# Attention, channel mix and gated MLP on one core: a reordered opening, and query features spread by DMA

## The chip, the cores and the metric

The kernel runs on one core of a Trainium2 chip. The metric is device time in microseconds of one execution. TensorE multiplies matrices, VectorE (DVE), ScalarE (ACT) and GpSimd (POOL) work on elements, and SyncE (SP) issues the DMAs of the kernel before.

## The reference

Three layers follow each other, for 4 batches of 1088 positions, in float32:

```python
# 1. linear attention, 4 heads of 32, r = 8
phi(x)[s, 8*i + j] = (S1 @ x[s])[i] * (S2 @ x[s])[j]      # 64 features per head
q_p, k_p = phi(q), phi(k)
kv = sum_s k_p[s, f] * v[s, d];   z = sum_s k_p[s, f]
x  = (q_p @ kv) / (q_p @ z + 1e-6)                        # heads side by side: 128 channels
# 2. channel mix
xk = mu_k * x + (1 - mu_k) * x_prev;   xr = mu_r * x + (1 - mu_r) * x_prev
x  = sigmoid(xr @ w_r) * (relu(xk @ w_k) ** 2 @ w_v)      # 128 -> 1024 -> 128
# 3. gated MLP with a mix over positions
h = relu(x @ w_in);  u, v = halves of h;  v_n = layernorm(v)
out = (u * (w_spatial @ v_n + b_spatial)) @ w_out
```

## The kernel before, in words

**Number formats.** Most large products are three fp32r matmuls: both factors are split in a high and a low part, and `mm3` (L111) multiplies low by high, high by high and high by low. An fp32 matmul on unsplit operands is one instruction in the program and two records in the profile. The weights arrive as 64-bit numbers; `load64` issues the load (L147) and `conv64` converts one piece to high and low parts with some five VectorE instructions (L124 to L129), two or three of ScalarE and one of GpSimd (L132). Three raw buffers take turns, so the fourth load waits for the first conversion.

**Chunks.** The 1088 positions of a batch are three chunks of 384, 384 and 320; `i` = 0 to 11 counts the chunks of all batches. Attention and channel mix go chunk by chunk, and the last layer follows per batch.

**Attention of a chunk.** `k_feat` computes key features: three fp32 matmuls of 128 positions (L188) give the two projections, with positions on partitions, and an outer product on VectorE or GpSimd (L199) gives 256 features. `k_sum` adds features times values over the nine tiles of a batch (L219; the mask is L224). `q_feat` does the same as `k_feat` for queries. `q_turn` transposes the features by six TensorE transposes (L240) and two ScalarE copies, so that features lie on partitions. `q_num` multiplies them with the key sums (L257) and divides (L261 to L263). `q_out` transposes back (L275). `prep` mixes a chunk with its shifted copy and splits it (L296 to L300), `prep_r` does so for the gate.

**Channel mix.** One step `g` is one of eight 128-wide pieces of a chunk: `up(g)` is an `mm3` and a ReLU (L339), `sqsplit(g-1)` the square, `down(g-4)` the down-projection. A piece is of one of two kinds: "P" squares on GpSimd (L342), makes the high part on ScalarE (L371) and the low part on VectorE, and needs an `mm3` in `down`; "D" squares on ScalarE (L359) and needs one fp32 matmul with the total of the value weights `wvT` (L385). Kinds alternate, P for even pieces. At a chunk's last piece VectorE multiplies by the gate (L389). 96 steps make up the loop; `plan(g, fn, ...)` hangs other work on a step: the features, turn, numerators and way back of chunk j at steps `QS[j]` and after (a new chunk every seven steps), key features of the next batch, weight loads and conversions.

**Order.** The program is traced in this order, and a planner that simulates the engines then sets each engine's order; `behind(anchors, fn)` makes all instructions of `fn` come after the given ones on the same engine. DMAs are issued by SP in order.

**The opening.** The loads go out in this order: the projections, keys of batch 0 (L166), the first half of the up-weights (L147), the first query chunk (L173), values of batch 0 (L177), constants, the second half of the up-weights, keys of batch 1, and so on. Eleven matmuls on zeros (L556) come first on TensorE. Then: key features of batch 0, features of query chunk 0, key sums, turn, numerators, way back, `prep(0)`, key features of batch 1 on GpSimd, key sums of batch 1, and the loop.

Of the kernel before, what the change touches and what calls it, by code (L numbers as in the profile page):

```python
# [12 lines left out]
ALU = mybir.AluOpType  # L13
# [18 lines left out]
CONVP = (512,)  # L32
NWARM = 11
VP = 2 * (HD + 1)
G1 = 26
WS = 30
WR = 2.5
C0 = 17
CS = 6
EARLY = 4  # L40
KB1 = ("w4", "w5", "w6")
QP = (3, 4, 6, 9, 10)
KP = (6, 10)
QJ = (0, 0, 4, 1, 0, -4, -1, 0, 2, 2, 0, -8)
PG = 1
ES = 93
EP = 2
# [12 lines left out]
ORD0 = ((0, 0), (1, 0), (0, 1), (1, 1), (2, 0), (3, 0), (2, 1), (3, 1), (0, 2), (1, 2), (2, 2), (3, 2))  # L60
R0 = (1, 4, 5)
R1 = 5
VW = NH * (HD + 1)
# [3 lines left out]
def attn_moe_gmlp(ctx: ExitStack, tc: tile.TileContext, qT, kT, va, st, wk, wv, wr, win, wout,  # L67
# [4 lines left out]
    pool = ctx.enter_context(tc.tile_pool(name="sb", bufs=1))  # L72
    pp = ctx.enter_context(tc.tile_pool(name="ps", bufs=1, space=PSUM))

    uid = [0]
# [128 lines left out]
    def k_feat(b, c, pb=4, eng=None):  # L204
        kp = kps[b, c] = sb((KB1 if b == 1 else ("n0H", "n0L", "n1H"))[c], [128, 3, 256])
        features(k_s[b], c, kp, pb, GE if 3 * b + c in KP else eng, eng is not None)

    def k_sum(b, g, ts=range(NT)):
        if g == 0 and ts[0] == 0:
            kps[b] = bank(3 if b == 1 else 5)  # L210
        kv = kps[b]
        v8 = v_s[b][0].rearrange("p t h c -> p t (h c)")
        v9 = v_s[b][1].rearrange("p h c -> p (h c)")
        wide = b % 2 == 0
        w = VW if wide else VP
        for t in ts:
            kp = kps[b, t // 3][:, t % 3, 128 * g:128 * g + 128]
            vt = v8[:, t] if t < NK else v9
            TE.matmul(kv[:, w * g:w * g + w], lhsT=kp, rhs=vt if wide else vt[:, VP * g:VP * g + VP],  # L219
                      start=(t == 0), stop=(t == NT - 1))  # L220
        if g == 1:
            nh = w // (HD + 1)
# [4 lines left out]
            kbd[b] = kb.rearrange("p (g h) c -> p g (h c)", g=2)  # L227

    def q_feat(i):
        qp = qst[i] = sb("n1L", [128, 3, 256])  # L230
        features(q_s[i // 3], i % 3, qp, 4, GE if i in QP else None)

    def q_turn(i):
        c = i % 3
        n = CH[c][1]
# [95 lines left out]
    def up(g):  # L331
# [6 lines left out]
        r = sb(rot(*R), [128, n])  # L338
        SE.activation(out=r, in_=hk, func=AF.Relu)  # L339
        if kind(g) == "P":  # L340
            sq = sb(rot(*R), [128, n])
# [7 lines left out]

    def kind(g):  # L350
        p = PAT[(g >= G1) + (g >= G2)]
        return p[g % len(p)]

    def sqsplit(g):
        i, f = divmod(g, NF)
        n = CH[i % 3][1]
        if kind(g) == "D":
# [19 lines left out]
    def down(g):  # L377
# [5 lines left out]
        w = slice(128 * f, 128 * f + 128)  # L383
        if kind(g) == "D":
            TE.matmul(vvs[i], lhsT=wvT[:, f // 2], rhs=hls.pop(g), start=f == 0, stop=f == NF - 1)  # L385
        else:
# [96 lines left out]
    def spatial(b, d, c, fill, early=False):  # L483
# [34 lines left out]
        def tail():  # L518
            mm3(po[c], woH[:, ds], woL[:, ds], gH, gL, rank == 1, rank == ND)
            if rank == ND:  # L520
# [28 lines left out]
    winH, winL = sb("winH", [128, DFF], F32R), sb("winL", [128, DFF], F32R)  # L549
    woH, woL = sb("woH", [128, DG], F32R), sb("woL", [128, DG], F32R)  # L550
    T2s = [sb(f"T2{d}", [128, 128], F32R) for d in range(ND)]
    zero = sb("mx", [128, CMAX], F32R)
    VE.memset(zero.bitcast(F32), 0.0)
# [20 lines left out]
    wseq += [(win, winH, winL, o, CV) for o in range(0, DFF, CV)]  # L574
    wseq += [(wout, woH, woL, o, CV) for o in range(0, DG, CV)]
    wi = [0]
# [17 lines left out]

    load64(*wseq[0])
    load_q(0, (0,))
    load_v(0)
    nc.sync.dma_start(out=idn, in_=ident)
    nc.sync.dma_start(out=mus[:, 0:2], in_=mu)
    VE.tensor_scalar(out=mus[:, 2:3], in0=mus[:, 0:1], scalar1=-1.0, scalar2=1.0, op0=ALU.mult, op1=ALU.add)  # L600
    load64(*wseq[1])
    load_k(1)
    load64(*wseq[2])
    load_v(1)
    load_q(0, (1, 2))
    for c in range(NCH):
        k_feat(0, c, c)
    k_last = outer[0]

    def behind(anchors, fn, *a):  # L610
        with ExitStack() as es:
            for x in anchors:
                es.enter_context(tc.issue_after(x.ins))
            fn(*a)

    q_feat(0)
    k_sum(0, 0)
    k_sum(0, 1)
    k_mask0 = list(k_mask)
    q_turn(0)  # L620
# [8 lines left out]
    k1_last = outer[0]  # L629
    behind([k_last], conv64)  # L630
    load64(*wseq[3])
    behind(nd_pe0, k_sum, 1, 0, range(3))
    behind(x_turn0, k_sum, 1, 0, range(3, NT))
    k_sum(1, 1)
    behind(k_mask0 + [k1_last], conv64)
    load64(*wseq[4])
    load_q(1)
# [6 lines left out]
    def gated(fn):  # L644
        return wraps(fn)(lambda *a: behind(prep_0, fn, *a))

    NI = B * NCH
# [12 lines left out]
    for b in range(1, B):  # L660
        last = QS[3 * b]
        ks = (3, 6, 8) if b == 1 else (last - 19, last - 12, last - 5)
        for c in range(NCH if b > 1 else 0):
            plan(ks[c], k_feat, b, c)
        if b > 1:
            plan(last + 1, k_sum, b, 0)
            plan(last + 2, k_sum, b, 1)
        if b + 1 < B:
# [8 lines left out]

    def total_wv(h):
        H, L = [x.bitcast(F32).rearrange("p (f two d) -> p f two d", two=2, d=128)[:, 2 * h:2 * h + 2, 1] for x in (wvH, wvL)]
        GE.tensor_tensor(out=wvT[:, 2 * h:2 * h + 2], in0=H, in1=L, op=ALU.add)  # L680
# [9 lines left out]
    plan(R1 + 1, receive, 0)  # L690
    plan(R1 + 2, gate, 0)
    for n, x in enumerate(wseq[5:]):
        plan(C0 - 2 + CS * n, load64, *x)
        plan(C0 + CS * n, conv_late)
# [27 lines left out]
    ds = slice(DG - 128, DG)  # L722
    GE.tensor_tensor(out=wo_last, in0=woH[:, ds].bitcast(F32), in1=woL[:, ds].bitcast(F32), op=ALU.add)
    at[0] = NI * NF + 1
# [86 lines left out]
```

## Time and profile before

| | |
|---|---|
| three runs | 474.67 us median, 473.85 to 474.92 |
| profiled execution | 475.52 us, its span 473.7 us |
| TensorE busy | 456.4 us, 96% |
| VectorE, ScalarE busy | 235.6 us (50%), 236.3 us (50%) |
| GpSimd busy | 189.9 us (40%) |
| first up-projection | at 27.12 us |

The profile's span is the time between the first and the last instruction that it shows. Busy times are sums over instructions; a matmul's end is modelled, so overlapping matmuls can hide small gaps. A line such as L111 is that of a helper and stands for many places; the names of its operands tell them apart.

### The profile page before, as it was taken

To read this page: it belongs to the slowest core of one execution; us is meant where nothing else is said; L and a number is where in the kernel's file an instruction comes from. 1 tells how busy PE (TensorE), PEld (TensorE's weight loads), DVE (VectorE), ACT (ScalarE), POOL (GpSimd) and SP (SyncE) were. 2 spreads that over 40 slices of the span, in tenths; PEclk is the share of its full clock that TensorE was granted. 3 is DMA by queue.
4 is the path that set the end of the run, shared out by engine and by line. 5 is a ranking of instruction groups with operands and counts; after the bars stand their busy time and mean duration, and the time that the engine had idled before them with its cause. 6 is when DMAs were issued, how large, how long until landed. Compare 5 with 4: busy or idle time off the path is not lost.

```text
span 473.7 us, 7304 instructions
## 1 busy us (share of the span) xinstructions
PE 456.4 (96%) x2754; PEld 433.4 (91%) x2754; DVE 235.6 (50%) x433; ACT 236.3 (50%) x569; POOL 189.9 (40%) x247
## 2 busy tenths in 40 slices
PE   6987999989999999999999999999999999999997
PEld 5976899788998898899999999999999999999996
DVE  3778748788477774437552335621335521212121
ACT  2464687886786866876435423432523442311111
POOL 2447545576475785456325503341213440200000
PEclk9899999999999999999999999999999999999999
DMA  7952200112200000022000000000100000100001
GB/s 239 335 192 91 92 1 19 33 35 77 66 19 0 2 0 1 0 72 80 26 17 18 0 15 0 1 2 0 48 1 1 1 1 0 48 1 0 1 1 47
DMA packets 12228, 18.77 MB, mean 40 GB/s; under 512 B 1761, under 2 KB 10785, under 8 KB 12193
## 3 DMA queue, kind: packets, MB, share of 16 engines
q1 hardware_dynamic: 12192, 18.31, 12.3%
q8 instruction: 21, 0.34, 0.3%
q14 instruction: 15, 0.11, 0.1%
HBM read 16.08 MB, written 2.23 MB: 39 GB/s over the span
## 4 chain that ended last, share of the span: by engine, by line
PE 71%; DVE 9%; ACT 6%; DMA 5%; POOL 4%; issue 3%; SPq 1%; POOLq 0%; DVEq 0%; ACTq 0%
PE p L111 59%; DMA st<-in_wT_dram 3%; PE p L385 3%; DVE w L117 3%; PE p L219 2%; PE p L257 2%; PE p L507 2%; PE p L508 2%; ACT m L339 2%; DMA xs0H<-in_va_dram 2%; PE p L188 1%; DVE w L127 1%; ACT w L114 1%; DVE m L117 1%; ACT w L371 1%
## 5 line engine op out<-in xcount | busy, mean ns | idle before, releaser
L512 DVE TENSOR_TENSOR m<-p,m 128x384 f32<-128x384 f32 (+1 forms) x43 | 22.9, 532 | 96.9 <-PE p L508 92.7
L111 PE MATMUL p<-m,k 128*128 128x384 f32 (+1 forms) x288 | 65.4, 347 | 2.7 <-ACT m L339 2.7
L342 POOL TENSOR_TENSOR m<-m 128x384 f32<-128x384 f32 (+1 forms) x48 | 41.3, 863 | 46.9 <-ACT m L339 43.2
L499 ACT ACTIVATE m<-p 128x384 f32<-128x384 f32 (+1 forms) x44 | 20.6, 469 | 77.2 <-PE p L111 73.4
L111 PEld LDWEIGHTS p<-m,k 128*128 128x128 f32 x288 | 47.8, 189 | 6.9 <-ACT m L339 3.7
L111 PE MATMUL p<-w,m 128*128 128x384 f32 (+1 forms) x288 | 52.3, 327 | 0.0
L111 PE MATMUL p<-w,k 128*128 128x384 f32 (+1 forms) x288 | 51.6, 327 | 0.0
L111 PE MATMUL p<-w,n1H 128*128 128x384 f32 (+1 forms) x192 | 48.7, 330 | 1.0 <-DVE x L512 1.0
L111 PEld LDWEIGHTS p<-w,m 128*128 128x128 f32 x288 | 48.1, 188 | 0.5
L111 PE MATMUL p<-w,n0H 128*128 128x384 f32 (+1 forms) x192 | 48.2, 329 | 0.0
L111 PEld LDWEIGHTS p<-w,k 128*128 128x128 f32 x288 | 47.9, 188 | 0.3
L339 ACT ACTIVATE m<-p 128x384 f32<-128x384 f32 (+1 forms) x96 | 42.9, 473 | 9.5 <-PE p L111 8.9
L117 DVE TENSOR_TENSOR w<-m,w 128x384 fp32r<-128x384 f32 (+1 forms) x44 | 33.4, 771 | 26.5 <-ACT w L371 21.7
L117 DVE TENSOR_TENSOR m<-m,m 128x384 fp32r<-128x384 f32 (+1 forms) x47 | 27.2, 578 | 28.8 <-ACT m L114 27.6
L111 PEld LDWEIGHTS p<-w,n1H 128*128 128x128 f32 x192 | 34.2, 188 | 2.4 <-DVE x L512 1.3
L453 POOL TENSOR_SCALAR rs<-mv 128x1 f32<-128x1 f32 x34 | 8.4, 246 | 66.0 <-DVE mv L452 65.1
L111 PEld LDWEIGHTS p<-w,n0H 128*128 128x128 f32 x192 | 34.2, 188 | 0.5
L385 PE MATMUL p<-w,wvT 128*128 128x384 f32 (+1 forms) x88 | 34.5, 474 | 0.1
L447 ACT ACTIVATE VR<-p 128x512 f32<-128x512 f32 x34 | 20.2, 597 | 27.7 <-PE p L111 27.6
L111 PE MATMUL p<-w,n0L 128*128 128x384 f32 (+1 forms) x96 | 31.5, 328 | 0.0
L111 PE MATMUL p<-w,n1L 128*128 128x384 f32 (+1 forms) x96 | 31.5, 328 | 0.0
L455 DVE TENSOR_SCALAR VR<-VR,mv,rs 128x512 f32<-128x512 f32 x34 | 21.1, 621 | 20.4 <-POOL rs L454 20.4
(193 smaller groups left out, 1042.9 us busy)
## 6 DMA issues: line engine op xcount, KB each, us to landing
st<-in_wT_dram SPq DMA_DIRECT2D x16, 192.0 KB, 2.4
w<-in_kT_dram SPq DMA_DIRECT2D x8, 192.0 KB, 4.5
w<-in_qT_dram SPq DMA_DIRECT2D x8, 192.0 KB, 3.9
out_dram<-m SPq DMA_DIRECT2D x8, 192.0 KB, 1.9
st<-in_wT_dram SPq DMA_DIRECT2D x8, 160.0 KB, 2.3
xs0H<-in_va_dram SPq DMA_DIRECT2D x2, 528.0 KB, 7.0
xs0L<-in_va_dram SPq DMA_DIRECT2D x2, 528.0 KB, 4.4
w<-in_wk_dram SPq DMA_DIRECT2D x2, 512.0 KB, 6.2
```

Source lines behind the costliest of these rows:

```text
L111: TE.matmul(out_ap, lhsT=l, rhs=r, start=first and n == 0, stop=last and n == 2)
L117: return eng.tensor_tensor(out=L, in0=src, in1=H.bitcast(F32), op=ALU.subtract)
L219: TE.matmul(kv[:, w * g:w * g + w], lhsT=kp, rhs=vt if wide else vt[:, VP * g:VP * g + VP], start=(t == 0), stop=(t == NT - 1))
L257: nd_pe[0] = TE.matmul(o.rearrange("p h c -> p (h c)"), lhsT=qt[g][:, cut(c, t)], rhs=kb[:, g], start=not wide or g == 0, stop=not wide or ...
L339: SE.activation(out=r, in_=hk, func=AF.Relu)
L342: anchor[2] = GE.tensor_tensor(out=sq, in0=r, in1=r, op=ALU.mult)
L385: TE.matmul(vvs[i], lhsT=wvT[:, f // 2], rhs=hls.pop(g), start=f == 0, stop=f == NF - 1)
L447: SE.activation(out=v, in_=pv, func=AF.Relu)
L455: VE.tensor_scalar(out=v, in0=v, scalar1=mv[:, 0:1], scalar2=rs, op0=ALU.subtract, op1=ALU.mult)
L499: SE.activation(out=u, in_=pu, func=AF.Relu)
L507: TE.matmul(acc, lhsT=T2, rhs=wtile(NK, c)[1], start=False, stop=False)
L512: VE.tensor_tensor(out=u, in0=acc, in1=u, op=ALU.mult)
```

## The change

It has three parts.

- **Opening.** The first query chunk and the values of batch 0 are asked for before the up-weights; keys and values of batch 1 come after four of the weight loads. Eight filler matmuls on zeros stand between the query features of chunk 0 and the key sums, twelve more behind the first transpose of the way back. The conversions of both up-weight and both value-weight pieces are done before the loop, each behind a step of the chain. Key features and key sums of batch 1 move from the opening into the loop (steps 4, 6 and 8 for the features), with VectorE for the outer product. The gate of chunk 0 is prepared at step 1 where it was step 5.
- **Unsplit squares in chunk 0.** All eight pieces use one fp32 matmul: even ones are squared by GpSimd ("G"), odd ones by ScalarE ("D"). The totals of the even value-weight pieces go to `wvE`, in the place of the output weights' high part, which are loaded and converted later.
- **Query features of chunks 3 to 11.** One matmul with a reordered projection gives all 64 + 32 values (both factors of four heads) of a chunk with positions along the free dimension; ScalarE copies them to SBUF and issues a DMA to a buffer in DRAM; SP issues six DMAs that read them back, each row repeated over eight partitions, as the two factors of all 256 features with features on partitions; one product on VectorE or GpSimd makes the features in the place where the turned ones stood. The spread is issued three steps earlier than the features were (for chunks 3 to 9; at their old step for 10 and 11) and is pinned behind the last square, split and low part of the loop on their engines.

```diff
+NFILL = (8, 12)
+KS1 = (4, 6, 8)
+SPREAD = 3
+QE_ = 3
-R0 = (1, 4, 5)
-R1 = 5
+R0 = 2
+R1 = 1
 ...
     def k_feat(b, c, pb=4, eng=None):
-        kp = kps[b, c] = sb((KB1 if b == 1 else ("n0H", "n0L", "n1H"))[c], [128, 3, 256])
-        features(k_s[b], c, kp, pb, GE if 3 * b + c in KP else eng, eng is not None)
+        kp = kps[b, c] = sb(("n0H", "n0L", "n1H")[c], [128, 3, 256])
+        features(k_s[b], c, kp, pb, GE if 3 * b + c in KP else None)
 ...
+    def q_order():
+        t = sb("T12", [128, 2, 2 * NH, 8])
+        for x in range(2):
+            GE.tensor_copy(t[:, x], Sb[:, :, 8 * x:8 * x + 8])
+        Sq[0] = t.rearrange("p s h i -> p (s h i)")
+
+    def q_spread(i):
+        b, c = divmod(i, 3)
+        o, n = CH[c]
+        e = rot(1, 0)
+        pq = bank(6 + e)[:, :n]
+        TE.matmul(pq, lhsT=Sq[0], rhs=q_s[b][:, o:o + n], start=True, stop=True)
+        y = vr(8, n)[:96]
+        copy(y, pq[:96])
+        fa = VR[:, 2 * e:2 * e + 2, :n]
+        fb = VR[:, 6:8, :n] if e else sb("n1L", [128, 2, n])
+        far = dp.tile([96, n], F32, tag=f"far{e}", bufs=1, name=f"far_{i}")
+        nc.scalar.dma_start(out=far, in_=y)
+        for h in range(NH):
+            r, g = 8 * h, h // 2
+            if h % 2 == 0:
+                nc.sync.dma_start(out=fa[:, g], in_=far[r:r + 16].unsqueeze(1).to_broadcast([16, 8, n]))
+            nc.sync.dma_start(out=fb[64 * (h % 2):64 * (h % 2) + 64, g],
+                              in_=far[64 + r:72 + r].unsqueeze(0).to_broadcast([8, 8, n]))
+        qst[i] = (fa, fb)
+
+    def q_prod(i):
+        fa, fb = qst[i]
+        (GE if i in QP else VE).tensor_tensor(out=fa, in0=fa, in1=fb, op=ALU.mult)
+        qst[i] = [fa[:, 0], fa[:, 1]]
 ...
+        if kind(g) == "G":
+            sq = sb(rot("w4", "w5", "w6", "w7"), [128, n])
+            anchor[2] = GE.tensor_tensor(out=sq, in0=r, in1=r, op=ALU.mult)
+            hls[g] = sq
+            return
 ...
     def kind(g):
+        if g < NF:
+            return "GD"[g % 2]
 ...
-        if kind(g) == "D":
-            TE.matmul(vvs[i], lhsT=wvT[:, f // 2], rhs=hls.pop(g), start=f == 0, stop=f == NF - 1)
+        if kind(g) in "DG":
+            TE.matmul(vvs[i], lhsT=(wvT if f % 2 else wvE)[:, f // 2], rhs=hls.pop(g), start=f == 0, stop=f == NF - 1)
 ...
-    load64(*wseq[0])
     load_q(0, (0,))
     load_v(0)
     nc.sync.dma_start(out=idn, in_=ident)
+    load64(*wseq[0])
+    load64(*wseq[1])
     nc.sync.dma_start(out=mus[:, 0:2], in_=mu)
-    VE.tensor_scalar(out=mus[:, 2:3], in0=mus[:, 0:1], scalar1=-1.0, scalar2=1.0, op0=ALU.mult, op1=ALU.add)
-    load64(*wseq[1])
-    load_k(1)
+    GE.tensor_scalar(out=mus[:, 2:3], in0=mus[:, 0:1], scalar1=-1.0, scalar2=1.0, op0=ALU.mult, op1=ALU.add)
     load64(*wseq[2])
-    load_v(1)
     load_q(0, (1, 2))
 ...
+    def busy(i, n):
+        p = bank(i)[:, :CMAX]
+        for x in range(n):
+            TE.matmul(p, lhsT=zero[:, :128], rhs=zero, start=x == 0, stop=x == n - 1)
+
     q_feat(0)
+    q_last = outer[0]
+    busy(7, NFILL[0])
+    behind([q_last], conv64)
+    load64(*wseq[3])
+    load64(*wseq[4])
+    load_k(1)
+    load_v(1)
     k_sum(0, 0)
     k_sum(0, 1)
     k_mask0 = list(k_mask)
+    behind(k_mask0, conv64)
     q_turn(0)
     q_num(0)
     nd_last0 = list(nd_last)
     nd_pe0 = list(nd_pe)
+    behind(nd_last0, conv64)
     q_out(0)
-    x_turn0 = list(x_turn)
+    behind(x_turn[:1], busy, 3, NFILL[1])
     prep(0)
-    for c in range(NCH):
-        k_feat(1, c, c, GE)
-    ...
-    k_sum(1, 1)
-    ...
+    behind(prep_L[:1], conv64)
     load_q(1)
 ...
-            plan(QS[j] + sp * n, gated(fn) if j < 3 and n == 0 else fn, j)
+            early = QE_ if SPREAD <= j < 10 and n == 0 else 0
+            plan(QS[j] + sp * n - early, gated(fn) if j < 3 and n == 0 else pinned(fn) if j >= SPREAD and n == 0 else fn, j)
 ...
-    for n in range(3):
-        plan(R0[n], conv_first)
-        if n < 2:
-            plan(R0[n], total_wv, n)
+    for n in range(2):
+        for odd in range(2):
+            plan(3 * n, total_wv, n, odd)
+    plan(R0, conv_first)
+    plan(QS[SPREAD] - QE_ - 3, q_order)
     plan(R1, prep_r, 0)
```

## Rows read from the trace of the kernel before

**Rows 1.** The page: busy time, share and instructions of each engine.

```profile
PE 456.4 (96%) x2754; PEld 433.4 (91%) x2754; DVE 235.6 (50%) x433; ACT 236.3 (50%) x569; POOL 189.9 (40%) x247
```

**Rows 2.** By stretch: length, busy (count) of PE, PEld, DVE, ACT, POOL, clock, DMA, GB/s.

```profile
30.00:40.00 10.00, 6.87 (x52) 6.26 (x51) 9.23 (x16) 9.28 (x22) 4.62 (x6) 1.00 0.44 131
...
80.00:100.00 20.00, 17.94 (x116) 16.06 (x114) 14.81 (x24) 15.61 (x41) 12.21 (x12) 1.00 0.14 40
100.00:120.00 20.00, 19.05 (x116) 16.23 (x117) 16.66 (x25) 16.09 (x41) 13.04 (x12) 1.00 0.23 65
```

**Rows 3.** TensorE's waits by releaser: us in total, times, longest.

```profile
PE p L111 <- ACT m L339: 2.7, 4, 1.3
...
PE p L240 <- DVE n1L L199: 1.7, 1, 1.7
PE p L275 <- DVE VR L263: 1.6, 2, 1.4
...
PE p L188 <- ACT sab L114: 0.9, 1, 0.9
PE p L240 <- POOL n1L L199: 0.7, 1, 0.7
```

**Rows 4.** The chain of waits, in order of time: start, us, what.

```profile
11.30 5.97 PE p L219 x36
...
45.99 0.52 PE p L111 x3
...
101.20 0.65 PE p L240 x6
101.85 0.67 PE p L188 x6
102.70 0.65 PE p L385 x2
...
125.66 0.54 PE p L385 x2
```

**Rows 5.** Timeline of TensorE in the opening: start, us, operation.

```profile
15.74 0.84 PE L219 MATMUL p<-xs0H,n0L 128*128 128x132 f32 x6
16.41 0.61 PE L219 MATMUL p<-xs0H,n1H 128*128 128x132 f32 x4
...
19.75 1.52 PE L257 MATMUL p<-kb,VR 128*128 128x132 f32 x12
...
25.14 1.95 PE L219 MATMUL p<-xs0L,w 128*128 128x66 f32 x16
26.92 0.39 PE L219 MATMUL p<-va,w 128*128 128x66 f32 x2
27.12 1.83 PE L111 MATMUL p<-m,k 128*128 128x384 f32 x9
```

**Rows 6.** Table by stretch of one microsecond in the opening.

```profile
8.00:9.00 1.00, 0.00 (x0) 0.00 (x0) 0.00 (x0) 0.00 (x0) 0.00 (x0) 1.00 1.04 378
...
12.00:13.00 1.00, 1.00 (x6) 1.00 (x6) 1.00 (x2) 0.00 (x0) 0.00 (x0) 0.50 0.98 301
```

**Rows 7.** The page's costliest groups: busy, mean ns of one, idle before.

```profile
L339 ACT ACTIVATE m<-p 128x384 f32<-128x384 f32 (+1 forms) x96 | 42.9, 473 | 9.5 <-PE p L111 8.9
```

**Rows 8.** Timeline of SP: start, us, DMA issue.

```profile
3.99 0.43 SPq L177 DMA_DIRECT2D xs0H<-in_va_dram  x1
```

**Rows 9.** DMA issues by form: KB each, us from issue to landing.

```profile
st<-in_wT_dram SPq DMA_DIRECT2D x16, 192.0 KB, 2.4
...
out_dram<-m SPq DMA_DIRECT2D x8, 192.0 KB, 1.9
```

**Rows 10.** SP's own waits from 30 to 220 us: total, times, longest.

```profile
SPq L147 <- DVE w L128: 14.3, 3, 8.0
```

**Rows 11.** Timeline of VectorE: the gating product of chunks 0 and 4.

```profile
57.44 0.56 DVE L389 TENSOR_TENSOR x<-p,m 128x384 f32<-128x384 f32 x1 [0.69 <-ACT m L328]
...
120.01 0.55 DVE L389 TENSOR_TENSOR x<-p,m 128x384 f32<-128x384 f32 x1
```

More of the change, by code (lines that the diff above doesn't have):

```diff
@@ L38 @@
 C0 = 17
+KS1 = (4, 6, 8)
 CS = 6
 EARLY = 4
-KB1 = ("w4", "w5", "w6")
 QP = (3, 4, 6, 9, 10)
@@ L73, in attn_moe_gmlp @@
     pp = ctx.enter_context(tc.tile_pool(name="ps", bufs=1, space=PSUM))
+    dp = ctx.enter_context(tc.tile_pool(name="dr", bufs=1, space=bass.MemoryType.DRAM))
     uid = [0]
@@ L204, in k_feat @@
     def k_feat(b, c, pb=4, eng=None):
-        kp = kps[b, c] = sb((KB1 if b == 1 else ("n0H", "n0L", "n1H"))[c], [128, 3, 256])
-        features(k_s[b], c, kp, pb, GE if 3 * b + c in KP else eng, eng is not None)
+        kp = kps[b, c] = sb(("n0H", "n0L", "n1H")[c], [128, 3, 256])
+        features(k_s[b], c, kp, pb, GE if 3 * b + c in KP else None)
     def k_sum(b, g, ts=range(NT)):
         if g == 0 and ts[0] == 0:
-            kps[b] = bank(3 if b == 1 else 5)
+            kps[b] = bank(5)
         kv = kps[b]
@@ L227, in k_sum @@
             kbd[b] = kb.rearrange("p (g h) c -> p g (h c)", g=2)
+    Sq = [None]
+    def q_order():
[26 more added lines that the diff above has]
+        qst[i] = [fa[:, 0], fa[:, 1]]
     def q_feat(i):
+        if i >= SPREAD:
+            return q_spread(i)
         qp = qst[i] = sb("n1L", [128, 3, 256])
@@ L233, in q_turn @@
     def q_turn(i):
+        if i >= SPREAD:
+            return q_prod(i)
         c = i % 3
@@ L356, in sqsplit @@
         n = CH[i % 3][1]
+        if kind(g) == "G":
+            return
         if kind(g) == "D":
@@ L518, in tail @@
         def tail():
-            mm3(po[c], woH[:, ds], woL[:, ds], gH, gL, rank == 1, rank == ND)
+            mm3(po[c], wo[0][:, ds], wo[1][:, ds], gH, gL, rank == 1, rank == ND)
             if rank == ND:
@@ L549, in attn_moe_gmlp @@
     winH, winL = sb("winH", [128, DFF], F32R), sb("winL", [128, DFF], F32R)
-    woH, woL = sb("woH", [128, DG], F32R), sb("woL", [128, DG], F32R)
+    wo = []
+    wvE = sb("woH", [128, NF // 2, 128])
     T2s = [sb(f"T2{d}", [128, 128], F32R) for d in range(ND)]
-    zero = sb("mx", [128, CMAX], F32R)
+    zero = sb(m(5), [128, CMAX], F32R)
     VE.memset(zero.bitcast(F32), 0.0)
@@ L574, in attn_moe_gmlp @@
     wseq += [(win, winH, winL, o, CV) for o in range(0, DFF, CV)]
-    wseq += [(wout, woH, woL, o, CV) for o in range(0, DG, CV)]
     wi = [0]
@@ L623, in attn_moe_gmlp @@
     nd_pe0 = list(nd_pe)
+    behind(nd_last0, conv64)
     q_out(0)
-    x_turn0 = list(x_turn)
+    behind(x_turn[:1], busy, 3, NFILL[1])
     prep(0)
-    for c in range(NCH):
-        k_feat(1, c, c, GE)
[L629 to L633, printed above, removed]
-    k_sum(1, 1)
-    behind(k_mask0 + [k1_last], conv64)
-    load64(*wseq[4])
+    behind(prep_L[:1], conv64)
     load_q(1)
@@ L645, in gated, with pinned @@
         return wraps(fn)(lambda *a: behind(prep_0, fn, *a))
+    def pinned(fn):
+        return wraps(fn)(lambda *a: behind([x for x in anchor if x is not None], fn, *a))
     NI = B * NCH
@@ L661, in attn_moe_gmlp @@
         last = QS[3 * b]
-        ks = (3, 6, 8) if b == 1 else (last - 19, last - 12, last - 5)
-        for c in range(NCH if b > 1 else 0):
+        ks = KS1 if b == 1 else (last - 19, last - 12, last - 5)
+        for c in range(NCH):
             plan(ks[c], k_feat, b, c)
-        if b > 1:
-            plan(last + 1, k_sum, b, 0)
-            plan(last + 2, k_sum, b, 1)
+        plan(last + 1, k_sum, b, 0)
+        plan(last + 2, k_sum, b, 1)
         if b + 1 < B:
@@ L676, in conv_first, with total_wv, load_wo @@
         late(conv64)
-    def total_wv(h):
-        H, L = [x.bitcast(F32).rearrange("p (f two d) -> p f two d", two=2, d=128)[:, 2 * h:2 * h + 2, 1] for x in (wvH, wvL)]
-        GE.tensor_tensor(out=wvT[:, 2 * h:2 * h + 2], in0=H, in1=L, op=ALU.add)
+    def total_wv(h, odd):
+        H, L = [x.bitcast(F32).rearrange("p (f two d) -> p f two d", two=2, d=128)[:, 2 * h:2 * h + 2, odd] for x in (wvH, wvL)]
+        GE.tensor_tensor(out=(wvT if odd else wvE)[:, 2 * h:2 * h + 2], in0=H, in1=L, op=ALU.add)
     def conv_late():
         behind(anchor[:1], conv64)
-    for n in range(3):
-        plan(R0[n], conv_first)
-        if n < 2:
-            plan(R0[n], total_wv, n)
-    plan(R1, prep_r, 0)
[L690 to L693, printed above, removed]
+    for n in range(2):
[3 more added lines that the diff above has]
+    plan(QS[SPREAD] - QE_ - 3, q_order)
+    plan(R1, prep_r, 0)
+    plan(R1 + 3, receive, 0)
+    plan(R1 + 4, gate, 0)
+    def load_wo():
+        wo.extend([sb("woH", [128, DG], F32R), sb("woL", [128, DG], F32R)])
+        load64(wout, *wo, 0, DG)
+    for n, x in enumerate(wseq[5:] + [None]):
+        if x is None:
+            plan(C0 - 2 + CS * n, load_wo)
+        else:
+            plan(C0 - 2 + CS * n, load64, *x)
         plan(C0 + CS * n, conv_late)
@@ L722, in attn_moe_gmlp @@
     ds = slice(DG - 128, DG)
-    GE.tensor_tensor(out=wo_last, in0=woH[:, ds].bitcast(F32), in1=woL[:, ds].bitcast(F32), op=ALU.add)
+    GE.tensor_tensor(out=wo_last, in0=wo[0][:, ds].bitcast(F32), in1=wo[1][:, ds].bitcast(F32), op=ALU.add)
     at[0] = NI * NF + 1
```

1 line of the change is left out of this document (removed).

## The prediction

> **What bounds the kernel now.** The shares come first: TensorE is busy 96% of the span, every other engine half of it or less [rows 1]. So work taken off TensorE counts, and work taken off another engine only where TensorE waits for it. The table by stretch says where that is: full stretches nearly everywhere, and three with less, 6.87 of 10 us from 30 to 40, 17.94 of 20 from 80 and 19.05 of 20 from 100; in the first VectorE is busy 9.23 of 10 [rows 2]. Then TensorE's waits by releaser: 4.9 us between the first MLP matmul and 45 us (1.7, 1.6, 0.9 and 0.7, for VectorE, ScalarE and GpSimd) and 2.7 us for the ReLU that reads the up-projection's bank [rows 3]. Last the chain of waits, which is mostly TensorE itself: its rows are the prices of a matmul in a full stream [rows 4]. The opening is another regime, a chain of dependent steps up to the first up-projection at 27.12 us [rows 5].
>
> **The change part by part.**
>
> *Query features of nine chunks (3 to 11).* Each loses three feature matmuls (six records, 0.67 us) and six transposes (0.65 us) [rows 4]. Each gains one fp32 matmul of 384 or 320 columns; the same form in the down-projection takes 0.65 and 0.54 us [rows 4]. Nine chunks, three of them of 320: 9 x 1.32 = 11.88 less 6 x 0.65 + 3 x 0.54 = 5.52, so **6.36 us** less for TensorE. The numerator matmuls, turns back and everything behind them stay. The elementwise product has the same 768 elements per partition and goes to the same engine as before, so I price it at no change; its operands now all lie in SBUF. ScalarE loses one small copy and one of two bank reads of about 0.47 us [rows 7] and gains one DMA issue, 0.43 us if it costs there what it costs on SP [rows 8]: about level.
>
> What the features now need is a way through DRAM, which no row shows as a whole. Bounds by rows: matmul 0.65, bank read 0.47 [rows 7], issue 0.43 [rows 8], a write to DRAM of 192 KB 1.9 [rows 9], six reads issued in turn by SP at 0.43 (2.6) [rows 8], the last landing 2.4 after its issue, as a 192 KB load does [rows 9]: 8.5 us. The lower end is without queueing of the six issues, about 6; the upper end adds the longest wait seen on SP for a buffer, 8.0 [rows 10], as SP takes its DMAs in order: 16.5. I take 8.5, nearest to the undisturbed rows. The lead is five steps of the loop for chunks 3 to 9 (spread three steps early, product two steps after the old place of the features). Four chunks of eight steps lie between the two gating products at 57.44 and 120.01 us, so a step is 62.6 / 32 = 1.96 us and the lead 9.8 us [rows 11]. So the product is not late, by about 1.3 us. Chunks 10 and 11 have two steps, 3.9 us, and are late at their place by 4.6; but their prep comes over ten steps later, and what stands behind the product on its engine is a split or a square of the MLP, which has three steps (5.9 us) until its down-projection. I cost the wait at nothing; the cover is that slack.
>
> How the reads of the second factor are cut decides how wide they run. Every load behind rows 9 has 128 or more rows on both sides; none is shown with a first dimension of eight. The Trainium skill (DMA: Bandwidth & Descriptors, section "Why a DMA increments its semaphore by 16 and not by 1") says that a transfer runs on the largest number of engines up to 16 that divides the outermost dimension of both sides; the source of the second factor has 8 there, so half the engines would carry it. By that page the four reads take an estimated 1 us more, the chain is 9.5 us and the margin almost gone; no run here shows it. By the full-width rows the sum stands as it is, and so it does by the page as long as the slack holds; it lowers the point from which the slower rival below decides by that 1 us.
>
> *Unsplit squares in chunk 0.* Four of its eight down-projections go from three fp32r matmuls (0.52) to one fp32 matmul (0.65) [rows 4]: **0.52 us more** for TensorE. VectorE loses four subtractions, ScalarE four squares; GpSimd makes the square in both versions, and two more totals of the value weights. This counts where VectorE is at 9.23 of 10 [rows 2], and I book it there, below.
>
> *The opening.* Three things come earlier. (a) Values and the first query chunk are now asked for ahead of the first up-weights: 512 KB less in front of them, at 378 GB/s [rows 6] 1.4 us. (b) The key sums ran at half clock: granted 0.50 from 12 us on, after a microsecond without any TensorE work at 8 [rows 6], and took 5.97 us [rows 4]; at the pace of the last of them (0.67 us for six records, from 15.74 to 16.41) 36 records take 4.0 [rows 5]. The values, whose landing ended the wait, now come sooner, and eight filler matmuls lie in the gap, so I take full clock and 2.0 us. (c) Between the end of the key sums (17.27) and the numerators (19.75) lie 2.5 us with batch 1's key features among them; now only the turn 0.65 and two reads of 0.47 with their gaps, some 1.8: 0.7 us. The first up-projection moves from 27.12 to 27.12 - 1.4 - 2.0 - 0.7 = 23.0. Behind the numerators I change nothing: batch 1's work on GpSimd is gone, a value-weight conversion on VectorE takes its place. The twelve fillers there (some 2 us at 0.17) lie in a wait for VectorE and ScalarE.
>
> But batch 1's key features (3 x 0.67), its key sums (36 records at the pace of 16 in the 1.78 us between 25.14 and 26.92: 4.0) [rows 5] and the query features of chunk 1 (0.67) had been done in the holes before 27.12; they are now 6.7 us to be done after 23.0. So at the same state TensorE stands at 29.7 instead of 27.1: 2.6 us behind. What pays for this are the 4.9 us of waits after the first up-projection [rows 3], which 6.7 us of ready work and a lighter VectorE can fill. Net 4.9 - 2.6 = 2.3 us gain if none is left, 2.6 us loss if all are. VectorE sheds four subtractions and part of the weight conversions but gains three key products; three of the four conversions still stand there. I take 1.8 us of waits left: **0.5 us gain**.
>
> *Moved or pinned without cost:* the output weights' load and conversion (needed only in the last stage), the receptance of chunk 0 four steps earlier, the constant of mu to GpSimd (idle then). Pinned spreads keep ScalarE and GpSimd in the written order. SP gets 54 more issues, 9 x 2.6 us over about 110 us, when it is idle most of the time; a weight load behind them is a few us late, with steps in hand.
>
> **Sum.** 6.36 - 0.52 + 0.50 = 6.34 us off the profiled execution's 475.52 (its span is 473.7, 1.8 lie around it): 469.2. That execution is 0.85 above the median of 474.67, so **468.3 us**.
>
> **Rivals.**
>
> 1. *The holes close.* The opening leaves no waits (1.8 us more) and the 2.7 us for the ReLU [rows 3] go with the bank reads and the transposes' waits: 468.3 - 4.5 = 463.8. For it: those waits stand where ScalarE and VectorE are busy about 16 of 20 us [rows 2]. Against: ScalarE sheds little, and TensorE now needs each bank sooner.
>
> 2. *The other engines become the bound from 50 to 150 us.* A chunk takes 15.6 us [rows 11], and TensorE would be done 0.7 sooner, while VectorE and ScalarE keep their load at 15 to 17 of 20 us [rows 2] and add to each other in chains. If half of the 6.36 turns into waits: 471.5. If the 2.6 us loss of the opening comes on top, 474.6, no change. Against: 80 to 85% is not full.
>
> 3. *Late spreads, slower.* SP takes its queue in order, and three conversions' loads each found it waiting for a buffer, 8.0 us the longest [rows 10]. If the six reads stand behind such a wait, the chain is 16.5, past lead and slack (9.8 + 5.9 = 15.7) by 0.8 us; the product then stops its engine, the split behind it comes late, and TensorE waits in order. It decides from 7.9 us of waiting in all nine chunks, where each costs 0.7 and the gain is gone; at 9 us, 1.8 x 9 = 16 less 6.3: about 484. For it: chunks 10 and 11 have a lead of 3.9 only. Against: buffers in the middle stages are asked for long before need, and 54 issues spread out.
>
> 4. *The opening does not do what it says:* the clock still falls to 0.50 through the key sums (2.0 back) and the values land no sooner (1.4 back): 468.3 + 3.4 = 471.7.
>
> **How the numbers follow.** The forecast (466 to 470.5) has 0.50, rival 1 0.19, rivals 2 and 4 together 0.21 (a third of it at no change or worse), rival 3 0.10. The page's half width moved rival 3 from 0.08 to that; without it the forecast has 0.52. Low end: rival 1, 463. High end: rivals 2 and 4, 473.8, with rival 3 and a part of rival 2 left out. A measurement of this kernel can tell about 0.2%, 0.95 us, from no change: faster 0.85, within it 0.07, slower 0.08.
>
> **What would show it.** The key sums at granted clock 1.00 from about 10 to 14 us; the first up-projection at 22 to 24; 4.9 us of waits behind it shrunk to about 2; TensorE with no six-record feature and transpose groups past chunk 2, one two-record group in their place, its busy time lower by about 6; no row in which TensorE waits for a product from a spread. It is wrong if the products on VectorE and GpSimd show waits for the DMA above 6 us each, if the waits for the ReLU grow past 6 us, or if the first up-projection stays past 26.

## The result, and the profile after

The changed kernel takes 477.03 us (median of 20 runs, 475.87 to 480.29) against 474.85 before (20 runs, 473.80 to 476.39): ratio 1.0054, 95% interval 1.0038 to 1.0071. It is slower, by 2.2 us, where 6.4 us less were forecast. The profiled execution took 475.88 us with a span of 474.1, only 0.4 us above the profiled one before, so the trace shows no more than a part of the loss. The five executions above 479 us had mean granted clocks of 0.986 to 0.993, the five below 476.2 had 0.992 to 0.996.

First the page's busy times of the changed kernel, to hold against [rows 1]:

```profile
PE 454.5 (96%) x2680; PEld 427.8 (90%) x2680; DVE 232.5 (49%) x431; ACT 231.1 (49%) x547; POOL 188.7 (40%) x249
```

TensorE is busy 1.9 us less. By the prediction's prices it should be 6.36 less for the spread, 0.52 more for the squares and some 3.5 more for twenty fillers, 2.3 less in all. This leaves out two effects of the clock that nearly cancel: the key sums no longer run at half clock (2.0 us less), and the stretch from 100 to 120 us runs at a clock of 0.91 (an estimated 1.8 more, 0.09 of 20 us). The number of matmul records fell from 2754 to 2680, as the edits make it (90 and 4 less, 20 more): the work went as priced. The span did not follow. The opening, as a timeline of TensorE:

```profile
9.95 0.84 PE L224 MATMUL p<-xs0H,n0H 128*128 128x132 f32 x6
...
13.77 0.39 PE L224 MATMUL p<-va,n1H 128*128 128x132 f32 x2
...
23.11 1.81 PE L116 MATMUL p<-m,k 128*128 128x384 f32 x9 [1.84 <-ACT bs L119]
```

The key sums run from 9.95 to 14.0 us, in 4.0 us where they took 5.97 [rows 4], and the first up-projection starts at 23.11 (forecast 23.0). The table by stretch (length, then busy us of PE, PEld, DVE, ACT, POOL, granted clock, DMA share, GB/s) shows what came behind:

```profile
20.00:30.00 10.00, 6.99 (x40) 5.79 (x39) 9.41 (x15) 6.64 (x17) 7.28 (x7) 1.00 0.56 202
30.00:40.00 10.00, 9.91 (x54) 7.48 (x52) 5.71 (x11) 6.27 (x16) 5.48 (x7) 1.00 0.53 160
...
60.00:80.00 20.00, 17.58 (x114) 15.59 (x113) 16.33 (x28) 12.62 (x32) 11.26 (x13) 1.00 0.14 44
80.00:100.00 20.00, 18.19 (x116) 16.30 (x115) 14.36 (x26) 15.61 (x39) 11.90 (x11) 1.00 0.26 77
100.00:120.00 20.00, 17.55 (x91) 14.49 (x89) 14.90 (x21) 14.91 (x38) 13.49 (x14) 0.91 0.35 104
```

The hole from 30 to 40 [rows 2] is closed. From 60 to 120 us TensorE is idle 6.7 us, against 3.0 before ([rows 2], and the row below, in which it was full), and from 100 to 120 its clock is granted at 0.91. The kernel before:

```profile
60.00:80.00 20.00, 20.00 (x136) 18.55 (x135) 13.13 (x21) 16.04 (x41) 10.22 (x11) 1.00 0.01 1
```

The waits of TensorE in the changed kernel, to hold against [rows 3]:

```profile
PE p L116 <- ACT m L381: 3.0, 4, 1.4
PE p L317 <- DVE VR L305: 2.3, 2, 1.1
PE p L116 <- ACT bs L119: 1.8, 1, 1.8
PE p L116 <- DVE w L122: 1.8, 3, 0.7
PE p L299 <- issue: 1.7, 1, 1.7
```

The waits for the turn and the features (L240, L188) are gone; in their place stand longer waits for the division behind the numerators (L305, 2.3 us where its L263 had 1.6), the MLP's low parts (L122) and the numerators themselves (L299). The spread of one chunk, followed from engine to engine, shows how: chunk 7, timelines of ScalarE's queue, SP, VectorE and TensorE.

```profile
99.68 0.31 ACTq L253 DMA_DIRECT2D far<-VR  x1
...
101.60 0.56 SPq L257 DMA_DIRECT2D VR<-far  x1
...
104.11 1.20 SPq L258 DMA_DIRECT2D VR<-far  x2
...
108.85 1.11 DVE L264 TENSOR_TENSOR VR<-VR 128x768 f32<-128x768 f32 x1 [1.21 <-DMA VR<-far]
...
110.06 0.46 PE L299 MATMUL p<-kb,VR 128*128 128x132 f32 x2 [1.69 <-issue]
```

The write is issued at 99.68, the six reads take SP from 101.60 to 105.3, the product starts at 108.85 after VectorE stood 1.21 us, and TensorE, whose next matmuls are these numerators, stands 1.69 us until 110.06. Right behind this wait its clock falls to half:

```profile
110.00:111.00 1.00, 0.94 (x5) 0.97 (x6) 1.00 (x1) 0.97 (x3) 1.00 (x2) 0.71 0.00 0
111.00:112.00 1.00, 1.00 (x7) 1.00 (x6) 1.00 (x2) 0.52 (x1) 1.00 (x1) 0.50 0.11 14
```

Over all nine products, the waits of VectorE and GpSimd in front of them (us, times); 12.2 us of them are for reads:

```profile
  DMA VR<-far: 10.1, 5
  PE p L436: 2.6, 1
  DMA n1L<-far: 2.1, 2
```

### The profile page after: what moved, and what is told of

Read it like the earlier page. It is cut to its first block, busy times and chain, and to the rows that moved or that the text cites. A ratio compares the mean times of both kernels' runs of the same rounds, so it can differ in the third digit from the quotient of the medians.

```text
span 474.1 us, 7259 instructions
## 1 busy us (share of the span) xinstructions
PE 454.5 (96%) x2680; PEld 427.8 (90%) x2680; DVE 232.5 (49%) x431; ACT 231.1 (49%) x547; POOL 188.7 (40%) x249
## 4 chain that ended last, share of the span: by engine, by line
PE 77%; DVE 8%; ACT 4%; issue 4%; POOL 3%; DMA 2%; SPq 1%; DVEq 0%; POOLq 0%; ACTq 0%
PE p L116 62%; PE p L436 4%; PE p L224 3%; PE p L299 2%; DVE w L122 2%; PE p L559 2%; PE p L558 2%; ACT m L381 1%; PE p L193 1%; DVE w L129 1%; DVE w L132 1%; DMA w<-in_qT_dram 1%; DVE w L133 1%; PE p L247 1%; DVE w L131 1%
## 5 line engine op out<-in xcount | busy, mean ns | idle before, releaser
L389 POOL TENSOR_TENSOR m<-m 128x384 f32<-128x384 f32 (+1 forms) x44 | 37.2, 850 | 31.2 <-ACT m L381 28.5
L122 DVE TENSOR_TENSOR m<-m,m 128x384 fp32r<-128x384 f32 (+1 forms) x47 | 26.9, 571 | 31.7 <-ACT m L119 27.4
L122 DVE TENSOR_TENSOR w<-m,w 128x384 fp32r<-128x384 f32 (+1 forms) x40 | 29.2, 744 | 25.4 <-POOL m L389 17.2
L502 DVE BATCH_NORM_STATS2 bn<-VR 128x6 f32<-128x512 f32 x34 | 23.3, 687 | 14.1 <-ACT VR L498 14.1
```

What stands on the lines that cost most here:

```text
L122: return eng.tensor_tensor(out=L, in0=src, in1=H.bitcast(F32), op=ALU.subtract)
L389: anchor[2] = GE.tensor_tensor(out=sq, in0=r, in1=r, op=ALU.mult)
L502: VE.bn_stats(out=bn, in_=v)
```

## The experiments

Theory L: the products wait for late reads. Rivals: B, the lighter TensorE is held up by the other engines; O, the opening loses; T, the traffic itself slows the engines; C, the clock in the opening; P, the pins; and later V, a form of B: VectorE's load around the weight conversions. Where a run below leaves out a part of the work, its results are not those of the reference. Ratios are to the kernel before, run on the same chip, with 95% intervals.

**The opening alone.**

```diff
-SPREAD = 3
+SPREAD = 12
```

> The changed kernel with the query features of all chunks as before (three feature matmuls and six transposes); opening and unsplit squares of chunk 0 stay. Theory L (late reads: the spread saves its 6 us of TensorE time, and the products' waits for their reads give it back) and theory B (bound by VectorE and ScalarE once TensorE is lighter) both put the opening at a small gain, 0.5 to 1 us by the two profiles: 473.5 to 475 against 474.85. Theory O (the opening itself costs: fillers, work moved behind the first up-projection) expects 477 or more, the whole of the loss.

475.72 us, ratio 1.0030 (1.0018 to 1.0042): the opening with chunk 0's squares costs 1.3 us, neither theory's number. The spread adds another 1.3 us to it instead of saving 6.4. In this profile (of an execution of 476.67 us) the clock fell behind the first fillers:

```profile
20.00:30.00 10.00, 7.39 (x32) 6.49 (x31) 9.41 (x15) 6.64 (x17) 7.58 (x7) 0.70 0.51 194
```

**The spread alone**, in the kernel before (`q_order`, `q_spread`, `q_prod`, the pins and the early steps, nothing else).

> The kernel before with the query features of chunks 3 to 11 spread by DMA, and nothing else changed. L and B: what is saved comes back as waits, 474 to 477, with the same waits of VectorE and GpSimd for the reads (about 12 us in all). O: 468 to 470, as the spread would be worth its 6 us with the old opening.

483.89 us, 1.0187 (1.0153 to 1.0221): worse than any theory had it. With the old opening TensorE waited up to 3.0 us for one product, and the clock was at 0.83 to 0.91 from 60 to 120 us.

**No reads.**

```diff
-        for h in range(NH):
-            ... nc.sync.dma_start(out=fa[:, g], in_=far[...])
-            nc.sync.dma_start(out=fb[...], in_=far[...])
+    GE.memset(VR[:, 0:8, :], 0.0)      # once, at the start
```

> The changed kernel without the 54 reads back from DRAM: the products multiply what lies in their places (zeros written once at the start), the write to DRAM stays. L: the waits for reads are gone and TensorE collects its saving, 468 to 471. B: the load of VectorE, ScalarE and GpSimd is unchanged, so within 1 us of the changed kernel, 476 to 478.

473.77 us, 0.9987 (0.9975 to 0.9998). The zeros put the first up-projection at 24.63, 1.5 us late, so some 472.3 without them: L's direction, but a third short of its amount (the 1.5 us are read from the trace, not tested).

**A longer lead.** Six steps first, then five.

```diff
-QE_ = 3
+QE_ = 6      # lead6;  5 in lead5
```

> The changed kernel with the spreads six steps early where they were three (chunks 3 to 9), so the lead is eight steps, 15 us, against a chain of some 10 us. L: the products of chunks 3 to 9 wait no longer, 470 to 473 (chunks 10 and 11 keep their short lead). B: no change, 476 to 478.

480.05 us, 1.0116 (1.0100 to 1.0132). Not to be read as lead: at six steps chunk 5's spread stands at step 12, one step ahead of chunk 3's numerators, and its reads land in the place that chunk 3's features still hold. So these numerators use other data, and a wait between the two is added.

> The changed kernel with the spreads of chunks 3 to 9 five steps early where they were three, so the lead is seven steps, some 13 us, against a chain of some 10 us; unlike with six steps, no read lands in a place whose old features are still to be used. L (late reads) gives back what leaving out the reads gave: 472.5 to 475. B (bound by the other engines) sees no change: 476 to 478.

478.39 us, 1.0065 (1.0039 to 1.0090). L's number is missed. The profile says why: the write of chunk 7 was issued 6 us earlier, at 93.59, and the product moved as far forward and waited again.

```profile
102.32 1.47 DVE L264 TENSOR_TENSOR VR<-VR 128x768 f32<-128x768 f32 x1 [1.50 <-DMA VR<-far]
```

The product is not pinned. That its place in VectorE's order follows the simulated landing of the reads, and that this comes earlier than the real one at both leads, is inferred from this move; the planner's own times are not on record.

**All transfers, nobody waits for them.**

```diff
-        (GE if i in QP else VE).tensor_tensor(out=fa, in0=fa, in1=fb, op=ALU.mult)
+        fo = sb("n1L", [128, 2, n])
+        (GE if i in QP else VE).tensor_tensor(out=fo, in0=<of wkH>, in1=<of wkL>, op=ALU.mult)
```

> The changed kernel with all its transfers, but the products multiply two weight tiles that lie in SBUF since the opening and write to a third place; nobody uses what the reads bring. L: no product waits, so as without the reads and without the 1.5 us that the zeros cost there at the start: 471.5 to 473.5. T (the traffic itself and SP's extra issues slow the engines): 476 to 478.

472.44 us, 0.9952 (0.9934 to 0.9971). T falls: the 54 reads cost nothing that shows as traffic (472.44 with them, some 472.3 without; the nine writes are in both). That the features depend on them costs 477.03 - 472.44 = 4.6 us. But TensorE still waits, from 60 to 120 us nearly as much as with the dependence (6.3 of 60 us idle against 6.7), so the traces do not show where the 4.6 us lie; this one is of an execution of 473.91 us, with a clock of 0.83 from 20 to 40 us:

```profile
60.00:80.00 20.00, 17.92 (x118) 15.86 (x116) 15.95 (x27) 14.00 (x36) 11.82 (x11) 1.00 0.18 57
80.00:100.00 20.00, 18.26 (x117) 16.56 (x117) 16.89 (x25) 16.58 (x39) 14.53 (x13) 1.00 0.29 84
100.00:120.00 20.00, 17.49 (x103) 14.54 (x101) 14.27 (x25) 14.51 (x37) 13.07 (x13) 1.00 0.39 109
```

**More fillers**, and **no pins**.

```diff
-NFILL = (8, 12)
+NFILL = (8, 22)
```

> The changed kernel with 22 filler matmuls behind the first transpose where it has 12, so TensorE works through the 1.8 us before the first up-projection. C (part of the loss is a clock that falls in the opening of some executions, as it did from 20 to 30 us in the profile with the opening alone): 0.5 to 1.5 us less than the changed kernel, 475.5 to 476.5. If the clock has no part: no change, 477.

476.88 us, 1.0037 (1.0016 to 1.0058): not told apart from 477.03.

```diff
-... gated(fn) if j < 3 and n == 0 else pinned(fn) if j >= SPREAD and n == 0 else fn, j)
+... gated(fn) if j < 3 and n == 0 else fn, j)
```

> The changed kernel without the pinning: the spreads' copies and issues come where the planner puts them. P (the pins hold ScalarE's copy until its place and so make the reads late): earlier reads, 473 to 476. Without a part for the pins: 476 to 479, as the planner may also put a copy in the way of a square.

481.62 us, 1.0121 (1.0089 to 1.0154). P falls: without pins all nine writes went out by 72.7 us, and the products still waited 10.3 us for reads. What the loss comes from is not shown: TensorE waited 3.2 us for squares (L410), but 2.1 of them at 113.4 us, long behind the last copy of a spread.

**The product pinned**, with the lead of the change and with five steps.

```diff
-pinned(fn) if j >= SPREAD and n == 0
+pinned(fn) if j >= SPREAD and n < 2
```

> The changed kernel with the product pinned too, behind the last square, split and low part of the loop, so the planner can't put it where it expects the read's landing. L (products wait for late reads): a place two steps behind the old place of the features leaves 9.5 us against a chain of 10.3: part of the waits go, 474 to 476.5. If the waits are not the planner's placing: no change, 477.

476.75 us, 1.0038 (1.0018 to 1.0059): with the short lead a pinned product is not told apart from 477.03, although the products wait only 3.1 us for reads where they waited 12.2. So the waits for reads can nearly go and the loss stay: the pinned product comes later, chunk 7's at 111.84 instead of 108.85.

> The same with the spreads five steps early. With five steps and a free product the product moved forward by the same amount (chunk 7's from 108.9 to 102.3 us) and waited as before. L with the pin: no product of chunks 3 to 9 waits for its read, 472.5 to 474.5. Otherwise 476 to 479.

476.17 us, 1.0033 (1.0016 to 1.0050). Now the reads are there: one product waits for them, 2.1 us, chunk 11's. The time hardly follows. TensorE is idle 4.1 us from 60 to 80 us, where VectorE makes two weight conversions (68.3 to 80.7), and 4.5 from 100 to 120, behind the third (95.3 to 98.8):

```profile
60.00:80.00 20.00, 15.88 (x100) 13.61 (x98) 16.79 (x28) 12.55 (x31) 10.33 (x10) 1.00 0.23 69
80.00:100.00 20.00, 20.00 (x130) 18.17 (x130) 15.48 (x25) 16.27 (x39) 14.32 (x13) 1.00 0.33 97
100.00:120.00 20.00, 15.50 (x84) 12.07 (x82) 15.09 (x21) 13.88 (x36) 13.25 (x14) 1.00 0.36 105
```

**No products.** The edit of the unused reads, with `qst[i] = [wkH[:, :n], wkL[:, :n]]` and no product at all.

> The changed kernel with all its transfers and without the nine products: the numerators of chunks 3 to 11 multiply weight tiles that lie in SBUF. B (what is left of TensorE's saving is lost to VectorE, ScalarE and GpSimd, whose rows hold TensorE up at 60 to 120 us): 2 to 4 us below the kernel with products that need no read (472.4), so 468.5 to 470.5. If these engines' load isn't it: 472 to 473.

472.81 us, 0.9961 (0.9944 to 0.9979), against 472.44 with them: B in the form "the products' load" falls.

**VectorE lighter, in two ways**, both on the pinned product with the longer lead. First, unsplit squares in chunks 1 and 2 too:

```diff
-        if g < NF:
+        if g < 3 * NF:
             return "GD"[g % 2]
 ...
     def conv_late():
-        behind(anchor[:1], conv64)
+        behind([x for x in anchor[:1] if x is not None], conv64)
```

The second part matters: where all squares are unsplit there is no low part yet to stand behind, so two of the three late conversions lose their place. The first line is without the edit, the second with it:

```profile
68.30 0.94 DVE L129 TENSOR_SCALAR w<-w 128x512 int32<-128x512 int32 x1
29.78 1.23 DVE L129 TENSOR_SCALAR w<-w 128x512 int32<-128x512 int32 x1
```

> Longer lead, pinned products, and unsplit squares in chunks 1 and 2 as well (eight more squares: TensorE 1.0 us more, VectorE eight subtractions of 0.55 to 1.7 us and ScalarE eight squares less). B: the lighter VectorE brings back more than the 1.0 us from 40 to 90 us, 470.5 to 473. If TensorE's load counts alone: 1 us above the kernel without this, 473.5 to 475.5.

474.87 us, 1.0001 (0.9985 to 1.0016): 1.3 us less although TensorE has 1.0 us more to do. VectorE's load has fallen from 60 to 100 us, by subtractions and by the two conversions that now stand at 30 to 41 us, and TensorE is full there. It is not from 20 to 40, where VectorE holds them:

```profile
20.00:40.00 20.00, 17.58 (x81) 14.48 (x79) 19.41 (x32) 13.90 (x33) 13.63 (x13) 0.83 0.45 158
60.00:80.00 20.00, 20.00 (x114) 16.49 (x113) 8.39 (x16) 13.05 (x34) 9.86 (x12) 1.00 0.47 143
80.00:100.00 20.00, 20.00 (x129) 18.14 (x128) 11.49 (x22) 14.58 (x36) 11.16 (x12) 1.00 0.28 87
100.00:120.00 20.00, 18.54 (x107) 15.97 (x106) 15.04 (x24) 16.39 (x42) 12.22 (x13) 1.00 0.36 104
```

The products wait 8.2 us for reads again, 4.5 of them chunk 5's on VectorE at 74.3 us, in a stretch in which TensorE is full. Second, the late conversions left out:

```diff
+    def conv_cheap():                    # in place of conv64 at steps 17, 23, 29
+        raw, n, H, L = pending_raw.pop(0)
+        copy(H, raw[:, :, 1].bitcast(F32)); copy(L, raw[:, :, 1].bitcast(F32))
```

> Longer lead and pinned products, and the three late weight conversions (two of the input weights, one of the output weights, some five VectorE instructions of 0.4 to 1.3 us each, in the loop at steps 17, 23 and 29) left out: two ScalarE copies take their place. V (VectorE is late around the conversions, and TensorE, lighter by the spread, waits for it at 60 to 120 us): most of the 8 us without TensorE work from 60 to 120 us goes, 470 to 473 against 476.2. If VectorE's load there isn't the cause: 475.5 to 476.5.

473.24 us, 0.9969 (0.9950 to 0.9988), 2.9 us less and just outside the range. From 80 to 120 us TensorE is full, the 4.5 idle microseconds of 100 to 120 among it. From 60 to 80 it is not, with VectorE at 10.10 of 20: nearly all of it is one wait of 3.99 us for a ReLU, which stands on ScalarE behind the copy of a later weight piece that had not landed. From 20 to 60 TensorE is idle 7.2 us where it was 2.7. The trace is of an execution of 474.86 us, 1.6 above the median:

```profile
60.00:80.00 20.00, 16.01 (x84) 14.21 (x83) 10.10 (x16) 11.22 (x30) 9.40 (x10) 0.83 0.52 154
80.00:100.00 20.00, 20.00 (x131) 18.48 (x131) 11.50 (x23) 14.66 (x36) 11.00 (x11) 0.99 0.21 65
100.00:120.00 20.00, 20.00 (x122) 17.92 (x121) 11.95 (x21) 14.48 (x38) 8.89 (x9) 1.00 0.27 84
```

**The same on the unused reads** (unsplit squares in chunks 1 and 2, with the two conversions set free).

> Products that need no read (472.4), with unsplit squares in chunks 0 to 2. V: the lighter VectorE gives back most of the 3 us of the TensorE saving that are still missing, less 1.0 us for the eight fp32 matmuls: 470 to 471.5. Otherwise 473 to 474.

476.40 us, 1.0029 (1.0010 to 1.0048), 4 us more instead of 1 to 2 less. From 60 to 80 us TensorE is full here too; the loss stands earlier, 7.2 us idle from 20 to 60 (3.3 without the edit), where VectorE is full with the two conversions:

```profile
20.00:40.00 20.00, 15.31 (x82) 12.10 (x81) 19.38 (x33) 14.54 (x33) 14.62 (x13) 1.00 0.49 162
```

So the edit moves VectorE's load as much as it takes it away. That this makes the 4 us is argued from the trace; no run keeps the conversions in their place with the unsplit squares.

**The opening alone, filled.** `SPREAD = 12` with `NFILL = (8, 22)`.

> The opening alone with 22 filler matmuls where it has 12. C (the 1.3 us that the opening alone costs are the clock, granted 0.70 from 20 to 30 us there): 474 to 475. If they are the waits and the work moved behind the first up-projection: 475.5 to 476.5.

476.46 us, 1.0041 (1.0020 to 1.0061). In this profile the clock stays up:

```profile
20.00:30.00 10.00, 8.71 (x52) 7.77 (x51) 9.38 (x15) 6.62 (x15) 6.58 (x7) 1.00 0.61 227
```

The time is no lower. That alone does not clear the clock, as the ten fillers also put the first up-projection 1.0 us later (23.83 against 22.82). But the two executions of the opening alone at a mean clock of 0.999 took 475.24 and 475.72 us, still above the 474.42 of the kernel before: C does not explain the 1.3 us.

**All mended.** Longer lead, pinned products, unsplit squares in chunks 0 to 2, 22 fillers; then the same without any spread, and with the spread for chunks 3 to 9 only (`SPREAD <= i < 10`).

> The best form so far (longer lead, pinned products, unsplit squares in chunks 0 to 2; 474.87) with 22 filler matmuls. C: the clock stays up from 20 to 40 us, where it was 0.83 in the profile: 472.5 to 474, below both kernels. Otherwise 474.5 to 475.5.

473.89 us, 0.9980 (0.9966 to 0.9995): below both kernels, by a hair. The products still wait 8.4 us for reads here, and TensorE is idle 2.3 us from 60 to 120 us.

> The best form (473.89) with the query features of all chunks as before: new opening with 22 fillers, unsplit squares in chunks 0 to 2, no spread. Tells what the mended spread is worth: if TensorE's 6.4 us are collected once VectorE is lighter and the products don't wait, 478 to 480.5; if the spread is worth nothing even so, 473.5 to 475.

477.89 us, 1.0083 (1.0066 to 1.0100).

> The best form with the spread for chunks 3 to 9 only; 10 and 11, whose lead is two steps and whose products waited in most profiles, take features and transposes again (TensorE 1.45 us more). L: their waits cost more than that, 472 to 473.5. If these waits are covered, as the prediction had it: 474.5 to 475.5.

473.24 us, 0.9987 (0.9972 to 1.0001): the intervals overlap, although TensorE has 1.45 us more to do. So the spread of chunks 10 and 11 saves nothing that shows; that waits for their late reads eat its saving agrees with this but is not shown.

## Why the prediction was wrong, point by point

*Right:* the bound, the prices of TensorE's work, the key sums at full clock, the first up-projection (23.11 for 23.0), and the waits left behind it (from 23.11 to 50 us TensorE is idle 2.5 us, where 1.8 were assumed). The first up-projection came out partly by luck: the numerators start at 15.07, 0.6 us sooner than the sum has them, and the way behind them takes 8.0 us, 0.7 longer than before. A small slip: of the 4.9 us of waits [rows 3] 0.2 stand behind 60 us, not between the first MLP matmul and 45.

*Wrong, and the step that decides: "I cost the wait at nothing; the cover is that slack."* Two sizes in it were low. SP takes 0.53 to 0.68 us to issue a read that repeats rows, not 0.43, so six take 3.7 us. The last landing was put at 2.4 us behind the last issue; where a read of the second factor comes last and its product waits for it (chunks 3, 4, 7, 8 and 9), the product starts 2.5 to 3.8 us behind the end of that issue. From ScalarE's issue of the write to the product it is 8.1 to 10.4 us for chunks 3 to 9 where the terms sum to 7.4. And the slack does not cover: a product is not met at its step, but where the order written by simulation put it, and numerators stand behind it in TensorE's own order, which the step left out. The dependence costs 4.6 us (`reads_unused`). How much of this is waiting and how much the product's later place, the runs do not separate; with the product pinned the waits nearly went and the time stayed (`pinprod`). Rival 3 named the products, but with a wait of SP as its mechanism and 7.9 us as its threshold; apart from the landing of the write, SP waited at most 2.7 us in front of a read of a spread, and no threshold was needed.

*Wrong: 6.36 us off TensorE taken as 6.36 us of time.* With no wait for reads the spread is worth 475.72 - 472.44 = 3.3 us. That is rival 2, at its price ("if half of the 6.36 turns into waits: 471.5"), to which I gave a part of 0.21. Which engine holds TensorE up shows in its idle time from 60 to 120 us. In the changed kernel and the variants with its opening, its spread and split squares in chunks 1 and 2 (`no_conv` apart), VectorE is busy 43 to 51 of these 60 us and TensorE idle 5.1 to 8.6. Where the edit of the unsplit squares has taken VectorE to 34 to 36, TensorE is idle 1.5 to 2.3, in `reads_unused_gd` too; ScalarE's load is the same in both groups (41 to 46 and 43 to 44 us). `no_conv`, with VectorE at 33.6, lies between with 4.0, the one wait named there. Without the spread VectorE's 48 us leave 2.1 idle (`open_fill`): it is the lighter TensorE that runs into VectorE.

The times say less than these waits, because the same edit moves two conversions to 30 to 41 us. With the longer lead and the pinned product it gains 476.17 - 474.87 = 1.3 us. Without the spread it costs 477.89 - 476.46 = 1.4 us, not for its fp32 matmuls: TensorE's busy time is 460.4 us against 461.2, and it is idle 6.8 us from 20 to 60 us where it was 2.1. Read the other way, the spread with longer lead and pins is worth nothing with split squares (476.17 against 475.72, 12 fillers) and 477.89 - 473.89 = 4.0 us with unsplit ones (22 fillers).

*Wrong: the opening and the squares of chunk 0 at level (0.50 - 0.52).* They cost 1.3 us (0.9 to 2.0 by the interval). The chain came out as forecast, and so did the balance behind it in the trace of the opening alone at full clock: in `open_fill` the way behind the first up-projection takes 450.6 us against 446.6 before, 4.0 more, where the terms add up to 6.7 - 3.1 + 0.5 = 4.1. One term was too large for a median: (b) takes 2.0 us for key sums at half clock, as in the profiled execution. Of 119 executions of the kernel before, 41 had a mean granted clock of 0.999 or 1, which leaves no room for four microseconds at half clock (these alone make 0.996), and their median is 474.0 us against 474.9 for the others. So a third of them had full clock there already, and full clock goes with 0.8 us rather than 2.0; the forecast also took off the 0.85 us by which the profiled execution was above the median. This could be most of the 1.3 us, but no run tests it, and what is left stays open.

The measured terms, 474.4 + 1.3 - 3.3 + 4.6 = 477.0, add up to the measured time by construction, since each is the step from one kernel to the next; the sum proves none of them. Each comes from kernels whose whole order was made anew: ten more fillers moved medians by 0.7 up, 0.2 and 1.0 down, and the unsplit squares on the unused reads by 4 against an expected gain. Differences of a microsecond between variants are therefore not causes by themselves. Taken by ratios, each to the kernel before on the same chip, the terms are 1.4, -3.7 and 4.8 us.

The Trainium skill's rule on the width of a transfer (DMA: Bandwidth & Descriptors, section "Why a DMA increments its semaphore by 16 and not by 1") could not be told from these rows. The chain is 0.7 to 3 us longer than the sum, of which SP's issues explain 1.1. Behind a last read of the second factor the product starts 2.5 to 3.8 us after the end of its issue, behind a last read of the first factor 2.2 (chunk 5): that is the direction of the rule, but it is one row, and other transfers run beside it.

## What to carry to other kernels

Work taken off the bounding engine is worth only what the next engine lets through: look at each stretch that loses work, and ask which engine is second there. Here VectorE was busy some three quarters of it, and about half of the saving was left. A result that comes by DMA has a chain from issue to use that is longer than bytes over rate; price it from rows of its own kind. Where a planner sets the order, look where it put the consumer: here more lead alone moved the product forward with the reads, and it waited again. And test the dependence apart from the traffic, by letting the transfers run and using other data. Last, look at what else an edit lets go: the two conversions that lost their place changed the stretch under test as much as the edit did.

## What the runs showed of the hardware that was not expected

A DMA issue that repeats rows held SP 0.53 to 0.68 us, most plain ones 0.33 to 0.43. A write of 144 KB to DRAM, six repeated reads and their landing took 8.1 to 10.4 us from the first issue to the first use. The 54 reads, 6.7 MB in all, cost no time that shows as traffic beside the kernel's own loads (`reads_unused`). GpSimd's product of two 768-wide operands in SBUF took 1.82 to 2.12 us, where the old one, with operands repeated from a small tile, took 1.51 to 1.84; VectorE's took 0.86 to 1.23, three of the four on 640 columns, where 0.95 was the rule at 768 with an operand in a bank.
